# A Fourier layer, a soft mixture of experts and a Mish feed-forward on one core: shrunk spectra put in order at PSUM, second-stage chunks set one by one, forward spectra turned on chip

## The chip, the cores and the metric

The kernel runs on one core of a Trainium2 chip. The metric is the device time of one execution in microseconds (us), the median over several. The core has five engines with an instruction stream each: TensorE (PE; its weight loads are shown as PEld), VectorE (DVE), ScalarE (ACT), GpSimd (POOL) and SyncE (SP), which here only issues DMAs. They tell each other by semaphores that a result is there or a buffer is free. Matrix products land in PSUM; the rest of the work lies in SBUF and, between stages, in DRAM.

## The reference

Three layers follow each other. x is 8 batches of 3072 positions by 256 features, in float32; the weights of the last layer are 64-bit.

```python
X = np.fft.rfft(x, axis=1)                      # layer 1, per batch
Yr = Xr @ w_r - Xi @ w_i + b_r
Yi = Xr @ w_i + Xi @ w_r + b_i
Yr = sign(Yr) * max(abs(Yr) - 0.01, 0)          # shrink, Yi likewise
y = np.fft.irfft(Yr + 1j * Yi)

logits = y @ phi                                # layer 2, 32 slots = 8 experts x 4
d = softmax over all 24576 positions of logits; slot_input = d.T @ y
slot_out = relu(slot_input @ w1) @ w2           # per expert
c = softmax over the 32 slots of logits; z = c @ slot_out

h = z @ w_in; g = h * tanh(softplus(h)); out = g @ w_out    # layer 3
```

## The kernel before

The transform of 3072 points is split in two stages, 64 x 48. Per batch, `stage1` multiplies x by the 64-point matrix in six pieces, the result goes to DRAM (`sdr`, `store_a`) and comes back by position (`bt`, `load_b`) as four groups of 8 frequencies each. A group is numbered k, 32 in all. For a group, `stage2` makes the second-stage products in six chunks (two halves h of the features; chunks of 3, 3 and 2 frequencies, p0 = 0, 3, 6). ACT rounds each chunk out of PSUM to the high part xh, DVE makes the rest xl. `linear` then takes six steps per group, (eh, m) with eh = 0, 1 and m = 0, 1, 2: six products each (high by high, low by high, high by low, over the two halves), which read all chunks of the group. The step m = 0 leaves a sum k1, copied out by ACT; for m = 1 and 2 DVE adds k1 to the products (p), ACT makes the two shrinking halves (cl and p again), and GpSimd (DVE in the last group) subtracts them into the shrunk spectrum yt. The tile p has two buffers, cl has one.

From yt come two things. `project` multiplies by phi (pp) and DVE turns the result (phat) for the inverse transform of the logits (`inv1` to `inv2`). `ytrans` transposes yt in 128 x 128 blocks for later (tr, copied to y), reading every sixth column. Once per batch the logits are reduced (`smax1` to `smax3`, `csoft1`, `cexp`, `csoft2`, on dx, cm, lg), the weights d go through a forward transform (`fwd1` makes dps and dm, `d_load` fetches it as dd, `fwd2` makes dt, `dturn` turns it to dh), and `slots` sums d.T @ spectrum (sps). The part c goes to DRAM (`ctrans`, c_d). In between, the 64-bit weights of layer 3 are converted to float32 in pieces (`conv`, on DVE and GpSimd). After the last batch come the experts (`Experts.run`) and the feed-forward part (`ffn`, the matmuls at L868 and L910).

The order is written out by hand: each piece of work is put into a list with a position, and the list is sorted. The position counts groups: linear step i of group k stands at k + i / 6. The table `PA` holds the other offsets:

```python
at(k + PA["s2"] + PA["s2d"] * i, stage2, k, h, p0)   # i-th chunk of group k
at(k + i / 6, linear, k, i // 3, i % 3)
at(k + PA["pj"], project, k)
```

Each engine then works strictly along its own part of that list. PSUM is a ring of eight tiles (`psp`) in this part of the program.

Of the kernel before, what the change touches and what calls it, by code (L numbers as in the profile page):

```python
# [21 lines left out]
NP = 32  # L22
# [9 lines left out]
def constants():  # L32

    n1 = np.arange(R1, dtype=np.float64)
    n2 = np.arange(R2, dtype=np.float64)
    f1 = np.zeros((R1, R1))
    t = np.zeros((96, NP, 96))
    w = 2.0 * np.pi / SEQ
    f1[:, 0], f1[:, 1] = 1.0, np.where(n1 % 2 == 0, 1.0, -1.0)
    for pos in range(47):  # L40
        k, r = (R1 * (pos + 1), 0) if pos < 23 else (R1 // 2 + R1 * (pos - 23), R2)
        a = w * np.mod(n2 * k, SEQ)
        t[r:r + R2, 0, pos] = np.cos(a)
        t[r:r + R2, 0, 48 + pos] = -np.sin(a)
    t[0:R2, 0, 47] = 1.0
    t[0:R2, 0, 95] = np.where(n2 % 2 == 0, 1.0, -1.0)
    for q in range(1, NP):
        ang = 2.0 * np.pi * np.mod(n1 * q, R1) / R1
        f1[:, 2 * q], f1[:, 2 * q + 1] = np.cos(ang), -np.sin(ang)
        for k2 in range(R2):  # L50
            a = w * np.mod(n2 * (q + R1 * k2), SEQ)
            sg = 1.0 if k2 < R2 // 2 else -1.0
            t[0:R2, q, k2] = np.cos(a)
            t[R2:96, q, k2] = np.sin(a)
            t[0:R2, q, 48 + k2] = -sg * np.sin(a)
            t[R2:96, q, 48 + k2] = sg * np.cos(a)
    fd = np.kron(f1, np.eye(2))
    sel = np.tile(np.eye(NS), (4, 1))
    m = np.arange(128).reshape(4, 4, 2, 4)
    order = m.transpose(1, 0, 2, 3).reshape(-1)  # L60
    big = np.concatenate([fd, fd.T[order], np.eye(128), sel, np.tile(f1, (2, 1))], axis=1)
    tt = t.transpose(2, 1, 0)
    t3 = np.concatenate([t[:, :, 0:48] + t[:, :, 48:96], t], axis=2)
    both = np.concatenate([t3.reshape(96, -1), tt.reshape(96, -1)], axis=1)
    return np.ascontiguousarray(big.astype(np.float32)), np.ascontiguousarray(both.astype(np.float32))
# [3 lines left out]
def body(ctx, tc, x, w_r, w_i, b_r, b_i, phi, w1, w2, w_in, w_out, cbig, ct, out, dbg=None, stop=False):  # L69
# [53 lines left out]
    cs_t = {}  # L123

    x_t, b_t, xh_t, xl_t, yt_t, y_t, pt_t, k1_t = {}, {}, {}, {}, {}, {}, {}, {}
    sdr, spt, ddr, ch, a_t = {}, {}, {}, {}, {}
    XC = 512
    na = N2 * D // XC

# [94 lines left out]
    def stage2(k, h, p0):  # L224
# [15 lines left out]
        nc.scalar.activation(out=xh, in_=ps, func=AF.Copy)  # L240
        nc.vector.tensor_sub(part(xl_t[k]), ps, xh.bitcast(F32))  # L241
        if g == 0 and p0 == 0:
            for t in (xh_t[k], xl_t[k]):
                nc.vector.tensor_copy(t[:, h, 3 * NC:3 * NC + 48].rearrange("p (a r) -> p a r", r=2),
                                      t[:, h, 95:144:48][:, None, :].to_broadcast([128, 24, 2]).bitcast(F32))

    def linear(k, eh, m):
        if eh == 0 and m == 0:
            pool, tag = (bp, "b") if k >= NK - 2 else (yq, "yq") if k >= NK - 4 else (ytp, "yt")
            yt_t[k] = pool.tile([128, 2, 8, 2, 48], F32, tag=tag, name="yt")  # L250
        xh, xl, yt = xh_t[k], xl_t[k], yt_t[k]
        src, (wh, wl) = ((0, wsp["a"]), (2, wsp["b"]), (1, wsp["c"]))[m]
        w, nq = (NC + 2, 9) if m == 0 and k % 4 == 0 else (NC, 8)
# [11 lines left out]
                nc.tensor.matmul(full[:, 0:48 * nq].rearrange("p (q f) -> p q f", f=48), lhsT=ww[:, h, es], rhs=spec(xx, h), start=n == 0, stop=n == 5)  # L265
                n += 1
        if m == 0:
            k1_t[eh] = lp.tile([128, NC + 2], F32, tag="k1", name="k1")
            nc.scalar.activation(out=k1_t[eh][:, 0:w], in_=ps, func=AF.Copy)
            if w > NC:  # L270
                cs_t[eh] = cs = sm.tile([128, 2, 2], F32, tag="cs", name="cs")
                for i, sc in ((0, 0.5), (1, -0.5)):
                    nc.scalar.activation(out=cs[:, i], in_=k1_t[eh][:, NC:w], func=AF.Relu, scale=sc, bias=half[:, i, eh:eh + 1])
            return
        ri = m - 1
        p = lp.tile([128, 8, 48], F32, tag="p", name="p")
# [697 lines left out]
```

## Time and profile before

| | us |
|---|---|
| median of 3 runs | 1934.07 (1930.87 to 1936.53) |
| the profiled execution | 1935.8 |
| its span, first to last instruction | 1934.0 |
| PE busy in the span | 1875.3 (97%) |
| DVE busy | 1163.1 (60%) |
| ACT busy | 860.5 (44%) |
| GpSimd busy | 195.3 (10%) |

The span has two parts. Up to about 676 us lie the layers 1 and 2 with the experts; from there on the feed-forward part runs, whose matmuls at L910 and L868 hold most of the chain that ended last. A busy share over the whole span says little of the first part: it has to be read stretch by stretch. In the rows further down, a line is `engine line operation out<-in`; idle time stands with the engine that waited and what ended the wait.

### The profile page before, as it was taken

How to read it: one execution, taken by the hardware profiler on the slowest of the kernel's cores; microseconds unless marked ns; L12 is line 12 of the kernel's file. 1: busy time of each engine (PE TensorE's matmuls, PEld its weight loads, DVE VectorE, ACT ScalarE, POOL GpSimd, SP SyncE). 2: the span in 40 equal slices, each digit the busy share in tenths (PEclk: the TensorE clock that was granted, in tenths of full speed). 3: DMA queues.
4: the chain of work that ended last, by engine and by line, in shares of the span. 5: the costliest groups of instructions: out<-in, count | busy, mean ns of one | idle time of the engine just before them, and what ended most of it. 6: DMA issues, size and time to landing. Idle time of an engine off the chain costs nothing.

```text
span 1934.0 us, 29831 instructions
## 1 busy us (share of the span) xinstructions
PE 1875.3 (97%) x12106; PEld 1569.4 (81%) x12106; DVE 1163.1 (60%) x1810; ACT 860.5 (44%) x1380; POOL 195.3 (10%) x247
## 2 busy tenths in 40 slices
PE   6899999998998899999999999999999999999999
PEld 4687787777887488888888888888888888888887
DVE  3355655655566476666666666666666666666665
ACT  2666666665754243333333333333333333333332
POOL 0333333332332000000000000000000000000000
PEclk9999999999999999999999999999999999999999
DMA  9867777775663920020020020002002001000000
GB/s 246 235 150 173 168 184 177 170 185 132 161 167 107 343 74 22 23 55 22 12 55 23 23 55 23 23 12 55 22 23 55 22 19 48 22 23 22 23 22 23
DMA packets 96905, 164.28 MB, mean 85 GB/s; under 512 B 28784, under 2 KB 58096, under 8 KB 94848
## 3 DMA queue, kind: packets, MB, share of 16 engines
q1 hardware_dynamic: 93808, 155.13, 29.2%
q0 software_dynamic: 1792, 4.76, 0.8%
q10 hardware_dynamic: 1168, 2.49, 0.5%
q8 instruction: 95, 1.56, 0.3%
q14 instruction: 42, 0.34, 0.1%
HBM read 98.78 MB, written 63.57 MB: 84 GB/s over the span
## 4 chain that ended last, share of the span: by engine, by line
PE 88%; DMA 4%; DVE 3%; ACT 2%; issue 2%; POOL 1%; SPq 0%; POOLq 0%; ACTq 0%; DVEq 0%
PE o L910 56%; PE h L868 9%; PE l L265 8%; PE s L233 6%; PE tr L318 2%; PE s L201 2%; DMA dd<-ddr 2%; DMA bt<-sdr 1%; PE pp L296 1%; DMA xc<-in_x_dram 1%; PE sps L496 1%; POOL yt L285 1%; PE dt L478 1%; ACT cl L283 1%; PE iu L307 1%
## 5 line engine op out<-in xcount | busy, mean ns | idle before, releaser
L910 PE MATMUL o<-whl,gh 128*128 128x512 f32 x3072 | 1082.9, 395 | 0.0
L910 PE MATMUL o<-whl,gl 128*128 128x256 f32 x3072 | 827.9, 280 | 0.0
L881 ACT ACTIVATE g<-h 128x1024 f32<-128x1024 f32 (+1 forms) x385 | 394.2, 1025 | 747.8 <-PE h L868 738.0
L910 PEld LDWEIGHTS o<-whl,gh 128*128 128x128 f32 x3072 | 566.5, 188 | 121.5
L910 PEld LDWEIGHTS o<-whl,gl 128*128 128x128 f32 x3072 | 578.5, 188 | 31.5
L894 DVE TENSOR_TENSOR gl<-g,gh 128x1024 fp32r<-128x1024 f32 x383 | 468.9, 1224 | 29.2 <-DVE gh L887 1.4
L887 DVE CAST gh<-g 128x1024 fp32r<-128x1024 f32 (+1 forms) x385 | 265.8, 690 | 352.6 <-ACT g L881 352.6
L868 PE MATMUL h<-ctt,mst 128*128 128x512 f32 x768 | 240.7, 394 | 1.5 <-ACT g L881 1.0
L233 PE MATMUL s<-tall,bt 96*128 96x144 f32 x1024 | 143.0, 301 | 23.0 <-DMA bt<-sdr 12.1
L233 PEld LDWEIGHTS s<-tall,bt 96*128 96x128 f32 x1024 | 138.6, 202 | 31.0 <-issue 26.4
L241 DVE TENSOR_TENSOR xl<-s,xh 128x432 fp32r<-128x432 f32 (+1 forms) x192 | 94.6, 550 | 113.6 <-ACT xh L240 113.3
L285 POOL TENSOR_TENSOR yt<-cl,p 128x384 f32<-128x384 f32 x124 | 125.2, 1010 | 352.6 <-ACT p L284 220.2
L868 PEld LDWEIGHTS h<-ctt,mst 128*128 128x128 f32 x768 | 121.0, 188 | 19.7 <-ACT g L881 1.8
L283 ACT ACTIVATE cl<-p,tup 128x384 f32<-128x384 f32 x124 | 76.3, 615 | 134.0 <-DVE p L277 98.1
L918 DVE TENSOR_TENSOR os<-o,os 128x256 f32<-128x256 f32 x192 | 76.5, 419 | 77.2 <-ACT os L917 77.2
L277 DVE TENSOR_TENSOR p<-l,k 128x384 f32<-128x384 f32 x128 | 70.6, 553 | 85.2 <-PE l L265 61.9
L240 ACT ACTIVATE xh<-s 128x432 fp32r<-128x432 f32 (+1 forms) x192 | 79.0, 503 | 36.7 <-PE s L233 36.3
L917 ACT ACTIVATE os<-o 128x256 f32<-128x256 f32 x192 | 73.4, 383 | 41.5 <-PE o L910 37.7
L284 ACT ACTIVATE p<-p,tlo 128x384 f32<-128x384 f32 x124 | 76.3, 615 | 4.0
L201 PE MATMUL s<-xc,f 64*64 64x512 f32 x384 | 56.6, 650 | 9.6 <-DMA xc<-in_x_dram 9.5
L318 PEld LDWEIGHTS tr<-cb,yt 128*128 128x128 f32 x384 | 55.4, 235 | 12.0 <-issue 4.5
L318 PE MATMUL tr<-cb,yt 128*128 128x128 f32 x384 | 62.2, 306 | 0.0
(187 smaller groups left out, 1392.1 us busy)
## 6 DMA issues: line engine op xcount, KB each, us to landing
sdr<-a SPq DMA_DIRECT2D x96, 256.0 KB, 3.8
bt<-sdr SPq DMA_DIRECT2D x32, 768.0 KB, 8.5
out_dram<-os SPq DMA_DIRECT2D x47, 512.0 KB, 2.6
xc<-in_x_dram SPq DMA_DIRECT2D x90, 256.0 KB, 5.4
ctt<-c_d SPq DMA_DIRECT2D x28, 384.0 KB, 7.0
w1t<-in_moe_w_dram SPq DMA_DIRECT2D x6, 1024.0 KB, 7.4
c_d<-chl SPq DMA_DIRECT2D x14, 384.0 KB, 2.8
w2t<-in_moe_w_dram SPq DMA_DIRECT2D x5, 1024.0 KB, 12.2
```

The lines of the kernel that those rows point to most:

```text
L201: nc.tensor.matmul(ps[h][64 * c:64 * c + 64], lhsT=f64[hs], rhs=t[hs, XC * c:XC * c + XC], start=True, stop=True, tile_position=(64 * h, 6 ...
L233: nc.tensor.matmul(ps[:, i], lhsT=b_t[k][:, p0 + i, h * 128:(h + 1) * 128], rhs=t_m[:, 8 * g + p0 + i, :], start=True, stop=True)
L241: nc.vector.tensor_sub(part(xl_t[k]), ps, xh.bitcast(F32))
L265: nc.tensor.matmul(full[:, 0:48 * nq].rearrange("p (q f) -> p q f", f=48), lhsT=ww[:, h, es], rhs=spec(xx, h), start=n == 0, stop=n == 5)
L283: nc.scalar.activation(out=cl, in_=p, func=AF.Relu, bias=tup[:, ri, eh:eh + 1])
L285: nc.gpsimd.tensor_sub(yt[:, eh, :, ri, :], cl, p)
L318: nc.tensor.transpose(ps[:, i, eh], yt[:, eh].rearrange("p q r f -> p (q r f)")[:, 2 * c + i::6], ident)
L868: nc.tensor.matmul(ps[:, i], lhsT=mst[:, f * 128:f * 128 + 128], rhs=ct_t[b][:, 4 * m:4 * m + 4].rearrange("p n t -> p (n t)"), start=True ...
L881: nc.scalar.activation(out=v(g), in_=v(h), func=AF.Mish)
L887: nc.vector.tensor_copy(v(gh), v(g))
L894: nc.vector.tensor_sub(gl, g, gh.bitcast(F32))
L910: nc.tensor.matmul(o, lhsT=a[:, i, ts], rhs=w, start=f == 0 and n == 0, stop=f == 15 and n == 1)
```

## The change

Three edits in one. First, the shrunk spectrum yt is laid out in the order in which `ytrans` reads it, six blocks of 128 columns in a row: the reads of the linear step's PSUM by ACT (k1) and DVE (p) take every sixth column (`split6`), GpSimd writes runs of eight into yt, `ytrans` reads 128 neighbouring columns, `project` reads runs of 16, and a table of constants changes its row order to match. The two extra columns (cs, and the bins in `stage2`) are now read from PSUM by ACT and DVE. Second, the six chunks of `stage2`, which stood as one block before the last linear steps of the group ahead, are placed one in front of each linear step. Third, for the batches before the last, `fwd1` turns its result by two DVE transposes and `d_load` by eight PE transposes with one ACT and one DVE copy, as the last batch did already; the DMA to DRAM and the DMA back are gone, and `d_load` stands a little later.

```diff
-    tt = t.transpose(2, 1, 0)
+    r = np.arange(16)
+    tt = t.transpose(2, 1, 0)[np.concatenate([6 * r + m for m in range(6)])]
...
         if g == 0 and p0 == 0:
-            for t in (xh_t[k], xl_t[k]):
-                nc.vector.tensor_copy(t[:, h, 3 * NC:3 * NC + 48].rearrange("p (a r) -> p a r", r=2),
-                                      t[:, h, 95:144:48][:, None, :].to_broadcast([128, 24, 2]).bitcast(F32))
+            bins = full.rearrange("p q r f -> p (q r f)")[:, 95:144:48][:, None, :].to_broadcast([128, 24, 2])
+            xh, xl = (t[:, h, 3 * NC:3 * NC + 48].rearrange("p (a r) -> p a r", r=2) for t in (xh_t[k], xl_t[k]))
+            nc.scalar.activation(out=xh, in_=bins, func=AF.Copy)
+            nc.vector.tensor_sub(xl, bins, xh.bitcast(F32))
+
+    def split6(t):
+        return t[:, 0:NC].rearrange("p (q f m) -> p m q f", q=8, m=6)
...
-            yt_t[k] = pool.tile([128, 2, 8, 2, 48], F32, tag=tag, name="yt")
+            yt_t[k] = pool.tile([128, 2, 6, 128], F32, tag=tag, name="yt")
...
         if m == 0:
-            k1_t[eh] = lp.tile([128, NC + 2], F32, tag="k1", name="k1")
-            nc.scalar.activation(out=k1_t[eh][:, 0:w], in_=ps, func=AF.Copy)
+            k1_t[eh] = lp.tile([128, 6, 8, 8], F32, tag="k1", name="k1")
+            nc.scalar.activation(out=k1_t[eh], in_=split6(full), func=AF.Copy)
...
-        p = lp.tile([128, 8, 48], F32, tag="p", name="p")
-        nc.vector.tensor_add(p.rearrange("p q f -> p (q f)"), ps, k1_t[eh][:, 0:NC])
-        cl = lp.tile([128, 8, 48], F32, tag="cl", bufs=1, name="cl")
+        o = yt[:, eh].rearrange("p m (q r f) -> p m q r f", q=8, r=2)[:, :, :, ri]
+        p = lp.tile([128, 6, 8, 8], F32, tag="p", name="p")
+        nc.vector.tensor_add(p, split6(full), k1_t[eh])
+        cl = lp.tile([128, 6, 8, 8], F32, tag="cl", bufs=1, name="cl")
+        pf, cf = (t.rearrange("p m q f -> p (m q f)") for t in (p, cl))
...
-            nc.scalar.activation(out=cl, in_=p, func=AF.Relu, bias=tup[:, ri, eh:eh + 1])
-            nc.scalar.activation(out=p, in_=p, func=AF.Relu, scale=-1.0, bias=tlo[:, ri, eh:eh + 1])
-            nc.gpsimd.tensor_sub(yt[:, eh, :, ri, :], cl, p)
+            nc.scalar.activation(out=cf, in_=pf, func=AF.Relu, bias=tup[:, ri, eh:eh + 1])
+            nc.scalar.activation(out=pf, in_=pf, func=AF.Relu, scale=-1.0, bias=tlo[:, ri, eh:eh + 1])
+            nc.gpsimd.tensor_sub(o, cl, p)
...
-            v = yt[:, eh].rearrange("p q r f -> p q (r f)")
+            v = yt[:, eh].rearrange("p m (q j) -> p q m j", q=8)
             for a in range(3):
-                nc.tensor.matmul(ps[32 * a:32 * a + 32], lhsT=ph[:, eh, :], rhs=v[:, :, 32 * a:32 * a + 32],
+                nc.tensor.matmul(ps[32 * a:32 * a + 32], lhsT=ph[:, eh, :], rhs=v[:, :, 2 * a:2 * a + 2],
...
-                nc.tensor.transpose(ps[:, i, eh], yt[:, eh].rearrange("p q r f -> p (q r f)")[:, 2 * c + i::6], ident)
+                nc.tensor.transpose(ps[:, i, eh], yt[:, eh, 2 * c + i], ident)
...
-        dm = cp.tile([128, 32, N2] if last else [128, N2, NS], F32, tag="st" if last else "chl", bufs=1 if last else 2, name="dm")
+        dm = cp.tile([128, 32, N2], F32, tag="st" if last else "chl", bufs=1 if last else 2, name="dm")
         for i in range(2):
             ps = psum([128, 12, NS], "dps")
             nc.tensor.matmul(ps, lhsT=f1, rhs=d[:, 12 * i:12 * i + 12], start=True, stop=True)
-            if last:
-                nc.vector.transpose(out=dm.rearrange("p q n -> p n q")[:, 12 * i:12 * i + 12], in_=ps)
-            else:
-                nc.scalar.activation(out=dm[:, 12 * i:12 * i + 12], in_=ps, func=AF.Copy)
-        if last:
-            ch[b, 0] = dm
-            return
-        ddr[b] = dram.tile([NP, 96, NS], F32, tag="ddr", bufs=2, name="ddr")
-        nc.sync.dma_start(out=ddr[b].rearrange("q (r n) s -> (q r) n s", r=4), in_=dm)
+            nc.vector.transpose(out=dm.rearrange("p q n -> p n q")[:, 12 * i:12 * i + 12], in_=ps)
+        ch[b, 0] = dm
...
         if b < NB - 1:
-            dd = cp.tile([96, NP, NS], F32, tag="dd", name="dd")
-            nc.sync.dma_start(out=dd, in_=ddr[b].rearrange("q p s -> p q s"))
-            ch[b, 0] = [dd[:, q] for q in range(NP)]
-            return
+            both = cp.tile([96, 2, 4, 128], F32, tag="dd", name="dd")
...
-            dd = yp.tile([96, 4, 128], F32, tag="y", name="dd")
+            dd = both[:, a] if b < NB - 1 else yp.tile([96, 4, 128], F32, tag="y", name="dd")
...
-PA = dict(..., s2=-1.1, s2d=0.0002, ..., dl=2.05, ...)
+PA = dict(..., s2=-1.03, s2d=1 / 6, ..., dl=2.2, ...)
```

What this does to the order shows best on the two engines that empty PSUM. The first place is DVE around the start of a group in the fourth batch: xl is the low part of a chunk of `stage2`, p the sum of a linear step, cva a step of `conv`, phat the turned projection. Before:

```order
L277 TENSOR_TENSOR p<-l,k_2767 128x384 x2
L241 TENSOR_TENSOR xl<-s_2809,xh 128x432
L241 TENSOR_TENSOR xl<-s_2815,xh 128x432
L241 TENSOR_TENSOR xl<-s_2821,xh 128x288
L241 TENSOR_TENSOR xl<-s_2826,xh 128x432
L241 TENSOR_TENSOR xl<-s_2832,xh 128x432
L241 TENSOR_TENSOR xl<-s_2838,xh 128x288
L544 TENSOR_SCALAR cva<-cvs 128x256
L546 SCALAR_TENSOR_TENSOR cva<-cvs,cva 128x256
L277 TENSOR_TENSOR p<-l,k_2853 128x384
```

And the same place now:

```order
L283 TENSOR_TENSOR p<-l,k_2774 128x384
L242 TENSOR_TENSOR xl<-s_2798,xh 128x288
L283 TENSOR_TENSOR p<-l,k_2774 128x384
L242 TENSOR_TENSOR xl<-s_2827,xh 128x432
L541 TENSOR_SCALAR cva<-cvs 128x256
L242 TENSOR_TENSOR xl<-s_2859,xh 128x432
L543 SCALAR_TENSOR_TENSOR cva<-cvs,cva 128x256
L283 TENSOR_TENSOR p<-l,k_2843 128x384
L306 STREAM_TRANSPOSE phat<-pp 96x256
L545 SCALAR_TENSOR_TENSOR cva<-cvc,cva 128x256
L242 TENSOR_TENSOR xl<-s_2910,xh 128x288
L283 TENSOR_TENSOR p<-l,k_2843 128x384
```

Where two p followed each other and six xl came in a block, each p now has an xl ahead of it. The second place is ACT at the same time: xh is the high part of a chunk, cl and p are the two shrinking halves, k the sum k1, a a piece of `stage1`. Before:

```order
L283 ACTIVATE cl<-p,tup 128x384
L284 ACTIVATE p<-p,tlo 128x384
L240 ACTIVATE xh<-s_2809 128x432
L240 ACTIVATE xh<-s_2815 128x432
L240 ACTIVATE xh<-s_2821 128x288
L240 ACTIVATE xh<-s_2826 128x432
L240 ACTIVATE xh<-s_2832 128x432
L240 ACTIVATE xh<-s_2838 128x288
L269 ACTIVATE k_2853<-l 128x386
```

And now:

```order
L290 ACTIVATE cl<-p,tup 128x384
L291 ACTIVATE p<-p,tlo 128x384
L241 ACTIVATE xh<-s_2798 128x288
L208 ACTIVATE a<-s_2804 128x512
L208 ACTIVATE a<-s_2805 128x512
L290 ACTIVATE cl<-p,tup 128x384
L291 ACTIVATE p<-p,tlo 128x384
L241 ACTIVATE xh<-s_2827 128x432
L274 ACTIVATE k_2843<-l 128x384
```

The block of six xh is gone; one xh stands behind each pair cl and p. The third place is DVE in the reductions of a batch, where dx, cm and lg are passes over 768 columns and st is a copy of the inverse transform. Before:

```order
L311 COPY st<-iu 128x8x24
L383 TENSOR_TENSOR dx<-lg,mb 128x768
L391 TENSOR_REDUCE cm<-lg 128x24
L392 TENSOR_TENSOR lg<-lg,cm 128x768
L277 TENSOR_TENSOR p<-l,k_3169 128x384 x2
```

And now:

```order
L242 TENSOR_TENSOR xl<-s_3150,xh 128x432
L318 COPY st<-iu 128x8x24
L390 TENSOR_TENSOR dx<-lg,mb 128x768
L398 TENSOR_REDUCE cm<-lg 128x24
L399 TENSOR_TENSOR lg<-lg,cm 128x768
L242 TENSOR_TENSOR xl<-s_3187,xh 128x432
L283 TENSOR_TENSOR p<-l,k_3176 128x384
L242 TENSOR_TENSOR xl<-s_3206,xh 128x288
L283 TENSOR_TENSOR p<-l,k_3176 128x384
L439 STREAM_TRANSPOSE dm<-dps 128x12x32 x2
```

The same passes now stand between two xl, and the two transposes dm are new on DVE behind them.

## Rows read from the trace of the kernel before

**Rows 1.** Stretches: length; busy us of PE, PEld, DVE, ACT, POOL; PE's clock; DMA.

```profile
178.40:551.90 373.50, 359.68 (x3035) 288.75 (x3030) 214.42 (x499) 243.88 (x501) 123.03 (x154) 0.98 0.68 172
252.40:324.80 72.40, 70.99 (x616) 56.74 (x609) 42.88 (x102) 48.76 (x101) 24.57 (x31) 1.00 0.71 175
551.90:676.00 124.10, 112.17 (x1065) 82.11 (x1057) 71.39 (x165) 55.80 (x110) 26.30 (x31) 0.97 0.57 199
676.00:1934.00 1258.00, 1253.01 (x6912) 1082.03 (x6912) 796.26 (x966) 465.72 (x581) 0.00 (x0) 1.00 0.10 31
```

**Rows 2.** Waits of PE up to 676 us: total, times, longest.

```profile
PE s L233 <- DMA bt<-sdr: 12.1, 3, 6.5
PE dt L478 <- DMA dd<-ddr: 9.9, 7, 2.5
...
PE s L233 <- ACT dm L435: 2.5, 5, 0.9
```

**Rows 3.** Timeline of PE: start us, us from first start to last end.

```profile
255.58 0.49 PE L413 MATMUL ctps<-cb,lg 128*128 128x128 f32 x3
255.91 0.70 PE L318 MATMUL tr<-cb,yt 128*128 128x128 f32 x4
...
270.74 1.89 PE L318 MATMUL tr<-cb,yt 128*128 128x128 f32 x12
272.38 0.42 PE L265 MATMUL l<-xh,ch 128*128 128x384 f32 x1
...
278.54 4.08 PE L233 MATMUL s<-tall,bt 96*128 96x144 f32 x32
282.36 0.43 PE L265 MATMUL l<-xh,ah 128*128 128x384 f32 x1
...
283.52 0.34 PE L265 MATMUL l<-xh,bh 128*128 128x384 f32 x1
...
658.30 1.16 PE L769 MATMUL htp<-cb,hs 128*128 128x128 f32 x8
```

**Rows 4.** Waits of SP's queue: total, times, longest.

```profile
SPq L440 <- ACT dm L435: 80.0, 7, 26.6
```

**Rows 5.** The tile dm: ns min/median/max; DVE's is the last batch's.

```profile
L433 DVE STREAM_TRANSPOSE dm<-dps x2: 1143/1152/1161, 635.9 to 636.9; 128x384 f32<-128x384 f32 x2
```

**Rows 6.** The tile dd in the last batch.

```profile
L458 ACT ACTIVATE dd<-td x1: 593/593/593, 638.8 to 638.8; 96x512 f32<-96x512 f32 x1
```

**Rows 7.** Timeline of ACT, around 320 us.

```profile
317.95 0.61 ACT L283 ACTIVATE cl<-p,tup 128x384 f32<-128x384 f32 x1 [1.11 <-POOL yt L285]
...
319.12 2.37 ACT L240 ACTIVATE xh<-s 128x432 fp32r<-128x432 f32 x6
...
325.09 0.61 ACT L283 ACTIVATE cl<-p,tup 128x384 f32<-128x384 f32 x1 [1.45 <-DVE p L277]
```

**Rows 8.** Timeline of DVE, the same stretch.

```profile
319.66 0.61 DVE L241 TENSOR_TENSOR xl<-s,xh 128x432 fp32r<-128x432 f32 x1 [2.55 <-ACT xh L240]
320.18 0.30 DVE L244 CAST xh<-xh 128x48 fp32r<-128x48 f32 x1
...
324.44 0.55 DVE L277 TENSOR_TENSOR p<-l,k 128x384 f32<-128x384 f32 x1
```

**Rows 9.** The tile lg: reductions of a batch on DVE.

```profile
L383 DVE TENSOR_TENSOR dx<-lg,mb x9: 544/952/961, 144.8 to 634.3; 128x768 f32<-128x768 f32 x7, 128x384 f32<-128x384 f32 x2
L391 DVE TENSOR_REDUCE cm<-lg x8: 928/942/946, 146.4 to 634.8; 128x24 f32<-128x768 f32 x8
...
L405 DVE TENSOR_TENSOR lg<-lg,cs__2511 x1: 958/958/958, 240.9 to 240.9; 128x768 f32<-128x768 f32 x1
```

**Rows 10.** The tile p: GpSimd's subtraction.

```profile
L285 POOL TENSOR_TENSOR yt<-cl,p x124: 983/1007/1215, 50.1 to 615.5; 128x384 f32<-128x384 f32 x124
```

**Rows 11.** DVE's copies out of PSUM: the tiles mst and y.

```profile
L853 DVE CAST mst<-mr x2: 682/687/692, 675.2 to 675.9; 128x512 fp32r<-128x512 f32 x2
...
L321 DVE COPY y<-tr x3: 675/676/692, 639.8 to 642.5; 128x512 f32<-128x512 f32 x3
```

More of the change, by code (lines that the diff above doesn't have):

```diff
@@ L125, in body @@
     x_t, b_t, xh_t, xl_t, yt_t, y_t, pt_t, k1_t = {}, {}, {}, {}, {}, {}, {}, {}
-    sdr, spt, ddr, ch, a_t = {}, {}, {}, {}, {}
+    sdr, spt, ch, a_t = {}, {}, {}, {}
     XC = 512
@@ L272, in linear @@
                 for i, sc in ((0, 0.5), (1, -0.5)):
-                    nc.scalar.activation(out=cs[:, i], in_=k1_t[eh][:, NC:w], func=AF.Relu, scale=sc, bias=half[:, i, eh:eh + 1])
+                    nc.scalar.activation(out=cs[:, i], in_=full[:, NC:w], func=AF.Relu, scale=sc, bias=half[:, i, eh:eh + 1])
             return
         ri = m - 1
-        p = lp.tile([128, 8, 48], F32, tag="p", name="p")
-        nc.vector.tensor_add(p.rearrange("p q f -> p (q f)"), ps, k1_t[eh][:, 0:NC])
-        cl = lp.tile([128, 8, 48], F32, tag="cl", bufs=1, name="cl")
+        o = yt[:, eh].rearrange("p m (q r f) -> p m q r f", q=8, r=2)[:, :, :, ri]
[3 more added lines that the diff above has]
+        pf, cf = (t.rearrange("p m q f -> p (m q f)") for t in (p, cl))
         if k == NK - 1:
-            nc.vector.tensor_scalar(cl, p, tlo[:, ri, eh:eh + 1], thi[:, ri, eh:eh + 1], op0=ALU.max, op1=ALU.min)
-            nc.vector.tensor_sub(yt[:, eh, :, ri, :], p, cl)
-        else:
-            nc.scalar.activation(out=cl, in_=p, func=AF.Relu, bias=tup[:, ri, eh:eh + 1])
-            nc.scalar.activation(out=p, in_=p, func=AF.Relu, scale=-1.0, bias=tlo[:, ri, eh:eh + 1])
-            nc.gpsimd.tensor_sub(yt[:, eh, :, ri, :], cl, p)
+            nc.vector.tensor_scalar(cf, pf, tlo[:, ri, eh:eh + 1], thi[:, ri, eh:eh + 1], op0=ALU.max, op1=ALU.min)
+            nc.vector.tensor_sub(o, p, cl)
+        else:
+            nc.scalar.activation(out=cf, in_=pf, func=AF.Relu, bias=tup[:, ri, eh:eh + 1])
+            nc.scalar.activation(out=pf, in_=pf, func=AF.Relu, scale=-1.0, bias=tlo[:, ri, eh:eh + 1])
+            nc.gpsimd.tensor_sub(o, cl, p)
         if m == 2 and k % 4 == 0:
             cs = cs_t.pop(eh)
-            nc.gpsimd.tensor_sub(yt[:, eh, 0, :, 47], cs[:, 0], cs[:, 1])
+            nc.gpsimd.tensor_sub(yt[:, eh, 5, 7:16:8], cs[:, 0], cs[:, 1])
     def project(k):
@@ L795, in run @@
                 nc.vector.tensor_copy(sot[:, h, 16 * g:16 * g + 16].rearrange("p (j i) -> p j i", i=SPE), src)
-PA = dict(y=20, s1=-5.89, s1d=0.3402, lb=-1.91, s2=-1.1, s2d=0.0002, pj=1.18, yt=2.24, ytd=0.0002, tu=0.482, i2=1.17, m1=1.17, m2=1.34, m3=1.51, f1=1.84, c1=1.58, ce=1.58, ds=2.47, dl=2.05, c2=2.57, f2=2.46, sl=3.2, rc=0.3, cx=3.24, cxd=0.0002, x0=-0.79, x1=0.05, ytl=1.05, x2=1.3, x3=2.7)
+PA = dict(y=20, s1=-5.89, s1d=0.3402, lb=-1.91, s2=-1.03, s2d=1 / 6, pj=1.18, yt=2.24, ytd=0.0002, tu=0.482, i2=1.17, m1=1.17, m2=1.34, m3=1.51, f1=1.84, c1=1.58, ce=1.58, ds=2.47, dl=2.2, c2=2.57, f2=2.46, sl=3.2, rc=0.3, cx=3.24, cxd=0.0002, x0=-0.79, x1=0.05, ytl=1.05, x2=1.3, x3=2.7)
 TAIL = {
```

## The prediction

> **What bounds it now.** I read the table of stretches first, then the waits of PE, then PE's timeline, and last the timelines of ACT and DVE in one place. From 676 us on, the feed-forward part runs with PE busy 1253.0 of 1258.0 us, and no edit reaches it [rows 1]. The time can change only before that. The first 95.7 us wait for inputs (PE's longest wait for bt, 6.5 us, is among them [rows 2]) and hold too little of the changed work to move it. From 178.4 to 551.9 us lie five batches of equal work, 373.5 / 5 = 74.7 us each, with PE busy 359.7 / 5 = 71.9; the quietest batch took 72.4 us with PE busy 71.0 [rows 1]. So PE is the bound there, and what it idles is known by name: 9.9 us for dd, 2.5 for dm, 12.1 for bt, of which 5.6 come after the first stretch [rows 2]. ACT is busy 243.9 / 5 = 48.8 us a batch, DVE 42.9. The reader is to see a full engine with two others that are two thirds full, and to ask whether those two stay free enough once their work is strung differently.
>
> **What PE saves.** In ytrans the stationary operand is read now with a step of six words. Twelve such transposes took 272.38 - 270.74 = 1.64 us, 0.137 each; three transposes of words in a row took 255.91 - 255.58 = 0.33, 0.11 each [rows 3]. The change gives ytrans 128 words in a row, so it should go at the second rate: 12 x 0.027 = 0.32 us a group, 1.3 a batch. Against this stand eight new transposes per batch (td), 8 x 0.11 = 0.9, with a little for the entry. Thirty-two second-stage matmul passes took 282.36 - 278.54 = 3.82 us in one block [rows 3]; cut in six they are the same passes, and a break costs at most a filling of the pipe (0 to 0.1 us, twenty more per batch; I take 0.2 us a batch in all). PE's own work stays at 71.0 - 1.3 + 0.9 + 0.2 = about 70.8 us a batch.
>
> **What PE no longer waits for.** The trip of dm through DRAM goes, its two DMAs leave SP's queue, and with them SP's wait of 80.0 us over seven batches for ACT's dm [rows 4], behind which the stores of a, the loads of xc and the loads of bt stood. All 9.9 us for dd go, and probably the 2.5 and the 5.6. What is late next: td waits for two DVE transposes that write with a step of 24 words, 2 x 1.15 us [rows 5], against two ACT copies before. Between dps and td PE has two chunks and two linear steps, 2 x (0.72 + 1.16) = 3.8 us (six passes of 0.12, and a step from 282.36 to 283.52 [rows 3]), with a stage-1 piece and a projection beside them; so td is covered as long as DVE comes to dm in time, and costs up to 2.3 us a batch if not. fwd2 then waits for one ACT copy (0.59 [rows 6]) and one DVE copy of as many words as y (0.68 [rows 11]), and has twelve transposes, a chunk and a step to hide them. ACT is thereby about even, DVE gets 2.3 + 0.7 = 3.0 us a batch more.
>
> **What the other engines pay.** Both work strictly in the order written. Before, DVE does two p in a row and then six xl; after, one xl stands ahead of every p, and on ACT one xh stands behind every pair cl, p. An m = 1 or 2 step is then a relay. DVE's p starts; ACT's cl starts 325.09 - 324.44 = 0.65 us later; cl and p together take 319.12 - 317.95 = 1.17; then xh; DVE's xl starts 319.66 - 319.12 = 0.54 after xh; the next DVE work starts 0.52 later [rows 7, 8]. Only then can the next p start: 0.65 + 1.17 + 0.54 + 0.52 = 2.9 us from p to p (a little less where the chunk is one of two columns instead of three), while PE needs 0.5 to 0.7 us for a chunk and 1.16 for a step. In each such step ACT idles from the end of xh to cl, about 0.14 + 0.5 + 0.65 = 1.3 us, sixteen times a batch: 20.6 us on top of its 48.8, together 69.4. Two places add to that. Where dx, cm and lg stand between two xl, three passes of 0.95 us each [rows 9] lie in the relay: +2.8. Where csoft2 stands (a reduction like cm, 0.94, and a product, 0.96 [rows 9], with st and the turns of dh), ACT has 0.9 us of its own work to do meanwhile: about +2.6. Sum: 74.8 us a batch, say 75, against 70.8 of PE.
>
> PE may run ahead of the relay in the middle of a group (eight PSUM tiles), but at a group's start its first step needs the last xl. At a step with nothing between, the last xl ends 0.65 + 1.17 + 0.54 + 0.4 = 2.8 us after the start of the p that it follows, and PE wants it after a chunk, a step, a chunk and four matmuls, 0.5 + 1.16 + 0.7 + 0.7 = 3.1; a lag of a few tenths is allowed there, and 1 to 2.5 us where a stage-1 piece or dps lies between. Time that the relay loses after csoft2 or smax3 is therefore not made up in the next group. I take 75 us.
>
> **Costs that no row shows.** GpSimd's subtraction writes runs of 8 words instead of 48. It takes 1.0 us now [rows 10]. The next cl waits for it (one buffer), but xh, xl and p lie between, 1.7 us: up to about half as much again costs nothing, and a gain would be worth nothing. I take 1.0. The reads of PSUM with a step of six words by ACT (k1) and DVE (p): the nearest row is the copy of mst, 512 words read with a step of four, 0.687 us on DVE, against 0.676 for as many in a row [rows 11]. I take no cost; the far end is a doubling, as for DVE's transpose with a strided output. The moving operand of project falls into runs of 16 words; it is timed by 256 columns in both, and I take nothing, with 0 to 0.1 us a group as bounds.
>
> [...]
>
> **The sum.** Relay: (75.0 - 74.7) x 6.6 batches from 95.7 to about 590 us = +2. From 551.9 to 676 us PE idles 124.1 - 112.2 = 11.9 us [rows 1]; there the last dd wait (2.5 [rows 2]) goes and some forty transposes are 1 us cheaper; with a little of the slower clock that followed the wait, -4.5. Together -2.5 us. The profiled execution took 1935.8 us, 1.7 over the median of the runs shown, so it becomes 1933.3, and the median about 1932.
>
> **Rivals.** (1) The relay is hidden: PE's other blocks (projections, transposes, slot sums) give ACT and DVE the time to catch up, and PE stays full. Then a batch takes 70.8 plus some 0.7 of waits that stay: (71.5 - 74.7) x 6.6 - 4.5 = -25.6, 1908 us. For it: ACT and DVE have over 23 us of idle time a batch. Against it: that idle time is not free, since 20.6 of ACT's is now bound in the relay.
> (2) Slower: the same relay, but with what I left out. The weights of the last layers are converted (conv) in steps that DVE and GpSimd pass to each other, and these stand in DVE's order too; PE's stops at group starts also bring the slower clock, as the granted 0.97 to 0.98 in the stretches with long waits shows, against 1.00 in the quietest batch [rows 1]. At 78 us a batch: 3.3 x 6.6 - 3 = +19, 1953 us. It decides from 76 us on.
> (3) Strided reads of PSUM take twice as long: 16 p of 0.55 us [rows 8] more per batch in the relay, 8.8 x 6.6 = +58, 1990 us. The row of mst speaks against it. [...]
> (4) The transposes do not get cheaper, because the step was not the reason: the eight htp, whose step is eight words, took 1.16 us with their drain, hardly more than a row of words would [rows 3]. In the relay's case this costs nothing but 1 us at the end, in rival 1 it costs 1.3 x 6.6 = 9 us: 1917. It shifts, and does not decide.
>
> **Chances.** Relay near 75 us: 0.42, own range 1920 to 1946. Rival 1 (with 4): 0.30. Rival 2: 0.23. Rival 3: 0.05. A measurement of this kernel tells about 0.3%, 6 us, from no change. Of the relay's 0.42 I give 0.14 to faster by more than that, 0.20 to no difference, 0.08 to slower. Faster 0.30 + 0.14 = 0.44, same 0.20, slower 0.08 + 0.28 = 0.36. The range must hold both neighbours: 1904 to 1956.
>
> **What will show it.** Right: tr at 0.11 us each; no dd wait and no wait of SP for dm; ACT waiting for DVE's p far more than now, DVE for xh after each pair; PE stopped at the start of groups by xl. If PE waits there for nothing and a batch takes 71 us, rival 1 holds. If p or k1 take 0.8 us and more, rival 3. I am wrong altogether if the first stage's end does not lie between 646 and 700 us.

## The result

The changed kernel took 1950.16 us (median of four runs, 1949.18 to 1950.89), the kernel before 1933.05 in the same comparison (four runs, 1930.87 to 1936.53). The ratio is 1.0087, interval 1.0069 to 1.0104: slower by 0.9%, where 1932 and rather faster than slower had been forecast. The time lies in the range (1904 to 1956); the direction is wrong. It is close to the 1953 us of the second rival, but by luck: that rival needed 78 us a batch, and a batch took 75.6.

The profiled execution took 1950.63 us (span 1948.8). To compare equal work, the stretches are cut at the same events in each kernel: the first slot-sum matmul of batch 0 and of batch 5 (0.6 us behind each), and 3.4 us ahead of the feed-forward's first o. For the kernel before these are the cuts of [rows 1]. Stretches of the changed kernel (start:end, length, busy us of PE, PEld, DVE, ACT and POOL, granted clock, DMA share, GB/s):

```profile
179.80:558.00 378.20, 363.45 (x3074) 282.40 (x3069) 226.14 (x506) 240.81 (x508) 123.33 (x155) 1.00 0.63 159
558.00:689.30 131.30, 117.71 (x1098) 84.14 (x1088) 76.34 (x173) 57.54 (x115) 26.36 (x31) 0.96 0.51 183
689.30:1948.80 1259.50, 1254.66 (x6911) 1083.13 (x6910) 795.77 (x965) 465.38 (x580) 0.00 (x0) 1.00 0.10 31
```

Against [rows 1] the five batches took 4.7 us more (378.2 - 373.5; 75.6 instead of 74.7 each), the end of the first part 7.2 more (131.3 - 124.1), the start 1.4 (179.8 - 178.4) and the feed-forward part 1.5. That is 14.8 us, the difference of the spans. The batches' granted clock rose from 0.98 to 1.00, so it is not the clock that lengthened them. PE's busy time there rose as well, from 359.68 to 363.45 us, though its matmuls got cheaper: the same ones take 351.36 in e1 below. So a part of the waiting stands in the busy time, and not only in the idle time.

The waits of [rows 2] for dd and dm, and that of [rows 4], are gone. PE now waits most of all for ACT's xh (engine, line, what it waited for: total, times, longest):

```profile
PE l L270 <- ACT xh L241: 15.4, 18, 1.8
```

What ACT and DVE wait for shows the relay. In the kernel before, ACT's cl waited for DVE's p, and DVE's xl for ACT's xh, for this long in all:

```profile
ACT cl L283 <- DVE p L277: 98.1, 72, 3.5
...
DVE xl L241 <- ACT xh L240: 113.3, 46, 11.8
```

In the changed kernel it is:

```profile
ACT cl L290 <- DVE p L283: 165.8, 117, 4.5
...
DVE xl L242 <- ACT xh L241: 218.5, 152, 11.4
```

One turn of it, on DVE around 400 us in the changed kernel (start us, us, what; in brackets the idle time before it and what ended it):

```profile
399.26 0.57 DVE L242 TENSOR_TENSOR xl<-s,xh 128x432 fp32r<-128x432 f32 x1
399.75 0.41 DVE L543 SCALAR_TENSOR_TENSOR cva<-cvs,cva 128x256 int32<-128x256 int32 x1
400.08 0.55 DVE L283 TENSOR_TENSOR p<-l,k 128x384 f32<-128x384 f32 x1
...
402.31 0.46 DVE L242 TENSOR_TENSOR xl<-s,xh 128x288 fp32r<-128x288 f32 x1 [1.09 <-ACT xh L241]
402.69 0.37 DVE L481 STREAM_TRANSPOSE dh<-dt 128x192 f32<-128x192 f32 x1
402.99 0.52 DVE L283 TENSOR_TENSOR p<-l,k 128x384 f32<-128x384 f32 x1
```

The same stretch on ACT:

```profile
400.72 0.61 ACT L290 ACTIVATE cl<-p,tup 128x384 f32<-128x384 f32 x1 [4.47 <-DVE p L283]
401.37 0.61 ACT L291 ACTIVATE p<-p,tlo 128x384 f32<-128x384 f32 x1
401.89 0.39 ACT L241 ACTIVATE xh<-s 128x288 fp32r<-128x288 f32 x1
403.60 0.62 ACT L290 ACTIVATE cl<-p,tup 128x384 f32<-128x384 f32 x1 [1.32 <-DVE p L283]
```

And PE in it, in the first linear step of a group:

```profile
400.59 0.34 PE L270 MATMUL l<-xh,al 128*128 128x384 f32 x1
402.33 0.44 PE L270 MATMUL l<-xh,ah 128*128 128x384 f32 x1 [1.41 <-ACT xh L241]
```

Read them together: p at 400.08, cl at 400.72, xh at 401.89, xl at 402.31, the next p at 402.99, 2.91 us in all. ACT has been idle 4.47 us before cl, since DVE stood in csoft2's work (the passes over lg that end ahead of the first row shown); its xh, whose matmuls had ended at 398.57 us, stands behind cl and p. So PE's fourth product of the step, the first that needs the second half of xh, stands 1.41 us. ACT kept to the order written: this xh could have run 3.3 us before 401.89 and did not.

### The profile page after: what moved, and what is told of

Same layout as the page of the kernel before. It is cut to its first block, busy times and chain, and to the rows that moved or that the text cites. A ratio compares the mean times of both kernels' runs of the same rounds, so it can differ in the third digit from the quotient of the medians.

```text
span 1948.8 us, 29919 instructions
## 1 busy us (share of the span) xinstructions
PE 1891.2 (97%) x12162; PEld 1566.1 (80%) x12162; DVE 1177.5 (60%) x1815; ACT 855.4 (44%) x1389; POOL 195.7 (10%) x247
## 4 chain that ended last, share of the span: by engine, by line
PE 73%; ACT 11%; DVE 8%; issue 3%; DMA 1%; POOL 0%; ACTq 0%; POOLq 0%; SPq 0%; DVEq 0%
PE o L907 55%; PE h L865 9%; ACT cl L290 3%; PE l L270 2%; DVE p L283 2%; ACT xh L241 2%; ACT p L291 2%; DVE xl L242 2%; ACT y L330 2%; PE s L234 1%; ACT a L208 1%; PE sps L493 1%; PE s L202 1%; PE pp L303 1%; PE tr L325 1%
## 5 line engine op out<-in xcount | busy, mean ns | idle before, releaser
L242 DVE TENSOR_TENSOR xl<-s,xh 128x432 fp32r<-128x432 f32 (+1 forms) x192 | 106.4, 555 | 218.7 <-ACT xh L241 218.5
L234 PE MATMUL s<-tall,bt 96*128 96x144 f32 x1024 | 168.7, 300 | 13.4 <-issue 6.3
L234 PEld LDWEIGHTS s<-tall,bt 96*128 96x128 f32 x1024 | 148.8, 197 | 37.6 <-issue 18.7
L241 ACT ACTIVATE xh<-s 128x432 fp32r<-128x432 f32 (+1 forms) x192 | 93.8, 490 | 27.3 <-PE s L234 27.3
L270 PE MATMUL l<-xh,ah 128*128 128x384 f32 (+1 forms) x128 | 53.7, 419 | 15.5 <-ACT xh L241 15.4
L208 ACT ACTIVATE a<-s 128x512 f32<-128x512 f32 x90 | 48.9, 596 | 16.3 <-PE s L202 8.4
```

The source lines that it names most:

```text
L234: nc.tensor.matmul(ps[:, i], lhsT=b_t[k][:, p0 + i, h * 128:(h + 1) * 128], rhs=t_m[:, 8 * g + p0 + i, :], start=True, stop=True)
```

## Experiments

Every kernel was timed against the kernel before in three rounds. Ratios have 95% intervals; the batch is a fifth of the stretch between the two slot-sum marks and the end is the stretch from the second mark on, both of the profiled execution.

| kernel | median us | ratio to before | batch | end |
|---|---|---|---|---|
| before | 1933 | 1 | 74.7 | 124.1 |
| changed | 1950.2 | 1.0087 (1.0069 to 1.0104) | 75.6 | 131.3 |
| e1 changed, chunks in a block | 1913.7 | 0.9894 (0.9880 to 0.9909) | 70.7 | 123.4 |
| e2 before, chunks spread | 1982.8 | 1.0253 (1.0227 to 1.0279) | 80.4 | 134.0 |
| e3 before, layout | 1929.3 | 0.9984 (0.9968 to 1.0001) | 73.3 | 123.5 |
| e4 before, turn on chip | 1918.0 | 0.9919 (0.9904 to 0.9934) | 71.8 | 120.7 |
| e5 changed, last four groups in a block | 1941.8 | 1.0040 (1.0026 to 1.0054) | 76.1 | 121.4 |
| e7 changed, cl later | 1915.5 | 0.9899 (0.9876 to 0.9922) | 71.9 | 121.8 |
| e8 changed, xl later | 1911.0 | 0.9875 (0.9852 to 0.9898) | 70.8 | 122.3 |
| e9 changed, less conv | 1933.2 | 0.9999 (0.9985 to 1.0013) | 73.3 | 125.9 |
| e10 xl later, less conv | 1909.0 | 0.9886 (0.9860 to 0.9912) | 70.4 | 120.8 |

**The three parts apart.** First the change without its spread:

```diff
-s2=-1.03, s2d=1 / 6
+s2=-1.1, s2d=0.0002
```

> The changed kernel with the second stage's six chunks of a group back in one block ahead of the last linear step of the group before (as in the kernel before); layout and on-chip turn stay. Theory A, the relay (chunk in front of every linear step ties ACT and DVE together and PE waits for them): ACT's waits for DVE's p fall from 165.8 us to about 100, PE's 15.4 us for xh go, and what remains is PE's own saving (32 x 0.32 - 7 x 0.9 = 4 us) and the waits for dd, dm and part of bt that the on-chip turn removed (up to 18 us): 1911 to 1925 us. Theory B, the turn on chip costs the time (two DVE transposes of 1.15 us, an ACT and a DVE copy, eight transposes per batch, in front of the forward transforms): the spread is innocent, 1942 to 1952 us. Theory C, the two share it: 1926 to 1941 us.

Then each part alone on the kernel before. The spread (e2):

```diff
-s2=-1.1, s2d=0.0002
+s2=-1.03, s2d=1 / 6
```

> The kernel before with one edit: the second stage's chunks one in front of each linear step; old layout, and the forward spectra still turned through DRAM. Theory A, the relay: it is slower than before by at least what the whole change lost, since nothing of the change's savings is there: 1950 to 1970 us, with ACT waiting for DVE's p 150 us or more. Theory B, the turn on chip: no loss, 1928 to 1938 us.

The layout (e3) is the diff of `tt`, `stage2`'s bins, `linear`, `project` and `ytrans`:

```diff
+            k1_t[eh] = lp.tile([128, 6, 8, 8], F32, tag="k1", name="k1")
+            nc.scalar.activation(out=k1_t[eh], in_=split6(full), func=AF.Copy)
...
-                nc.tensor.transpose(ps[:, i, eh], yt[:, eh].rearrange("p q r f -> p (q r f)")[:, 2 * c + i::6], ident)
+                nc.tensor.transpose(ps[:, i, eh], yt[:, eh, 2 * c + i], ident)
```

> The kernel before with the layout alone: spectra ordered by part where PSUM is read (k1, p), runs of 128 words for the transposes of yt; chunks in a block, turn through DRAM. 384 transposes at 0.11 instead of 0.137 us are 10 us of PE's time. Theory A (PE bounds the blocked kernel): 1921 to 1927 us. If the gain is hidden behind the waits for bt and dd instead: 1930 to 1936 us.

The turn on chip (e4) is the diff of `fwd1` and `d_load`, with their new place:

```diff
-        dm = cp.tile([128, 32, N2] if last else [128, N2, NS], F32, tag="st" if last else "chl", bufs=1 if last else 2, name="dm")
+        dm = cp.tile([128, 32, N2], F32, tag="st" if last else "chl", bufs=1 if last else 2, name="dm")
...
-dl=2.05
+dl=2.2
```

> The kernel before with the on-chip turn alone (DVE transposes for dm, PE transposes and copies for dd, the last step placed at 2.2 as in the changed kernel); chunks in a block, old layout. Theory A, the relay is the loss and the turn a gain: the waits for dd (9.9 us), dm (2.5) and part of bt (5.6) go, 7 x 0.9 us of transposes come: 1918 to 1930 us. Theory B, the turn is the loss: 1945 to 1955 us.

Theory A holds in e1, e2 and e4, though e2 lies 13 us above its range. In e1 ACT's wait for p falls to 90.2 us and DVE's for xh to 94.1. The turn alone is worth 15 us, with the layout on top 19 (e1); the spread costs 36 us on top of both (1950.2 - 1913.7) and 50 alone. In the spread without the turn the DRAM trip takes part in the loss; PE's wait for dd was 9.9 us over seven times before [rows 2], and is in e2:

```profile
PE dt L478 <- DMA dd<-ddr: 25.7, 6, 6.0
```

The layout alone is between the two expectations and cannot be told from nothing (its interval reaches 1.0001). In the batches its PE time is there, though: from e4 to e1, where PE is no longer stopped by the trip, a batch falls by 1.1 us, as 48 transposes at 0.027 less would have it (1.3). In all, e1 is 4.4 us ahead of e4 and not 10, since its end is 2.7 us longer; why was not looked into. In e3 PE waits 12.9 us in all for dd, against 9.9 before, which takes a part of the gain.

e1's five batches, the same columns as above, show the full PE that the prediction had counted at 70.8 us a batch (353.6 / 5 = 70.7):

```profile
175.60:529.20 353.60, 351.36 (x3075) 280.81 (x3069) 226.99 (x502) 240.27 (x505) 123.76 (x154) 1.00 0.67 170
```

**The loop itself.** e1 takes away the relay and the chunks' place at once. Two kernels keep every chunk where the change has it, and every operation, and open the loop at one link each. In e7 cl, p and yt of a step follow the next chunk's xh on ACT:

```diff
+            def rest():
                 nc.scalar.activation(out=cf, in_=pf, func=AF.Relu, bias=tup[:, ri, eh:eh + 1])
                 nc.scalar.activation(out=pf, in_=pf, func=AF.Relu, scale=-1.0, bias=tlo[:, ri, eh:eh + 1])
                 nc.gpsimd.tensor_sub(o, cl, p)
...
+            late.append(rest)
```

> The changed kernel, chunks spread as there, with one thing moved: cl, p and GpSimd's subtraction of a linear step are issued behind the next chunk's high part (ACT: xh, cl, p instead of cl, p, xh). No work is added or removed. Now xh never waits for DVE's p, so the loop p, cl, p, xh, xl, p is open. Theory A, it is the loop that costs: most of the 36 us between the spread and the blocked form come back, 1910 to 1925 us, and ACT's waits for p and DVE's for xh fall by half or more. Theory B, it is the chunks' place as such (PE changes operand every few matmuls, and a chunk's xh and xl are needed sooner after they are made): 1940 to 1952 us.

In e8 xl follows the next p on DVE:

```diff
-        nc.vector.tensor_sub(part(xl_t[k]), ps, xh.bitcast(F32))
+        late.append(lambda: nc.vector.tensor_sub(part(xl_t[k]), ps, part(xh_t[k]).bitcast(F32)))
+        if k <= 0 or h == 1 and p0 == 6:
+            flush()
...
         nc.vector.tensor_add(p, split6(full), k1_t[eh])
+        flush()
```

> The loop opened at the other link: the changed kernel with a chunk's xl issued on DVE behind the next p instead of ahead of it (the last chunk of a group keeps its place, since the next linear step needs it). Theory A, the loop costs: a good part comes back, less than by the other link, because one step in six still has the old order: 1915 to 1932 us. Theory B, the place of the chunks as such: 1940 to 1955 us, since xl comes later.

Both give back all of it, e8 a little more than expected (1911.0). The chunks' place is innocent: theory B falls. DVE of e8, at the place shown above for the changed kernel:

```profile
376.79 0.56 DVE L295 TENSOR_TENSOR p<-l,k 128x384 f32<-128x384 f32 x1 [0.15 <-PE l L281]
377.26 0.60 DVE L242 TENSOR_TENSOR xl<-s,xh 128x432 fp32r<-128x432 f32 x1
...
379.03 0.46 DVE L242 TENSOR_TENSOR xl<-s,xh 128x288 fp32r<-128x288 f32 x1 [0.58 <-ACT xh L241]
379.41 0.37 DVE L494 STREAM_TRANSPOSE dh<-dt 128x192 f32<-128x192 f32 x1
379.70 0.52 DVE L295 TENSOR_TENSOR p<-l,k 128x384 f32<-128x384 f32 x1
```

p at 376.79 waits for PE alone, behind the same csoft2, and xl comes after it. From p to p it is still 2.91 us here, because this chunk is the group's last and keeps the old order; but ACT got its p one xl earlier, and PE runs through. The stretch of e8, with PE busy 353.6 of 354.2 us:

```profile
170.50:524.70 354.20, 353.55 (x3075) 282.15 (x3070) 229.49 (x506) 242.01 (x506) 125.37 (x154) 1.00 0.66 169
```

In part the expectation missed: that both waits fall by half. One link opened frees the engine behind it, the other keeps waiting where it costs nothing. In e7 ACT's wait for p falls to 39.2 us, DVE's for xh stays at 184.7:

```profile
ACT cl L299 <- DVE p L291: 39.2, 35, 2.0
...
DVE xl L242 <- ACT xh L241: 184.7, 128, 12.3
```

and in e8 it is the other way round:

```profile
ACT cl L303 <- DVE p L295: 112.9, 106, 2.2
...
DVE xl L242 <- ACT xh L241: 75.4, 71, 12.0
```

e7 is left with 71.9 us a batch. What its profile has more of is PE's wait for yt ahead of the projection, since cl comes later (in the changed kernel this row is 1.9 us, four times):

```profile
PE pp L314 <- POOL yt L301: 8.8, 10, 1.6
```

**The end.** e5 spreads groups 0 to 27 and puts only the last four in a block:

```diff
-            at(k + PA["s2"] + PA["s2d"] * i, stage2, k, h, p0)
+            at(k - 1.1 + 0.0002 * i if k >= NK - 4 else k + PA["s2"] + PA["s2d"] * i, stage2, k, h, p0)
```

> The changed kernel with the chunks spread for groups 0 to 27 and in one block for the last four groups (28 to 31) alone. From the last batch's first linear step to the feed-forward's first matmul the changed kernel took 122.2 us, the one with all chunks in a block 113.5. Theory A, the loss at the end is the relay in groups 28 to 31: 1938 to 1945 us. Rival: the end loses because ACT and DVE arrive there late, from the batches before: 1947 to 1953 us.

Theory A: the time lies in its range, and the end falls from 131.3 to 121.4 us, while the batches stay at 76. So the loss at the end is made there, in groups 28 to 31, not brought along.

**conv.** e9 takes four of conv's five steps on DVE and one of its two on GpSimd away:

```diff
-            p.tensor_tensor(c.bitcast(F32), hf, hf, op=ALU.mult)
...
-        elif step == 2:
+        elif step < 6:
+            return
+        elif step == 2:
...
-            p.tensor_tensor(c.bitcast(F32), a.bitcast(F32), c.bitcast(F32), op=ALU.add)
+            p.tensor_tensor(c.bitcast(F32), a.bitcast(F32), a.bitcast(F32), op=ALU.add)
```

> The changed kernel with less of conv: of its five steps on DVE four are left out (0.42 + 0.42 + 0.29 + 0.42 us) and of GpSimd's two one (0.61), so the converted weights are not the right ones. That is 1.55 us of DVE's work for each of 32 pieces, 50 us in all, four pieces a batch. Theory A, conv lies in DVE's waits for xh (117 us between 200 and 550): 1943 to 1951 us, the end a few us better. Rival (conv in DVE's order is part of the loop, piece by piece): up to 6 us a batch, 1910 to 1930 us; half of it: 1930 to 1940 us.

It is 17 us faster: theory A is refuted, and the time lies in the rival's middle case. A batch gains 2.3 us (75.6 to 73.3) and the end 5.4. Whether that is conv's own cost or its place in the loop, e10 tells, the same cut in the open loop of e8:

> The kernel with the loop opened on DVE (xl behind the next p) and with less of conv, the same steps left out as in the run on the changed kernel (so the converted weights are not the right ones). There conv's 50 us of DVE work were worth 17 us. Theory A, conv cost that time because it stood in the loop of p, cl, p, xh and xl: with the loop open PE is the bound and DVE's work is free, 1906 to 1912 us, no more than 4 us under the open loop's 1911. Rival, conv costs on its own account (ports, DMAs, DVE's load): again 12 us or more, 1890 to 1899 us.

There it is worth nothing that can be told: 1909.0 against 1911.0, with ratios to before of 0.9886 (0.9860 to 0.9912) and 0.9875 (0.9852 to 0.9898); the intervals leave room for some 5 us. So conv costs little or nothing by itself; its 17 us hang on the loop. The place above, around 400 us, shows how. There conv's L543 stands on DVE between xl and p, p starts 0.33 us later for it (399.75 to 400.08), and PE's stop is 1.41 us. In e9, which leaves that step out, the same stop is 0.37 us shorter:

```profile
393.61 0.45 PE L270 MATMUL l<-xh,ah 128*128 128x384 f32 x1 [1.04 <-ACT xh L241]
```

Not every wait of conv reaches PE. Around 590 us in the changed kernel, first GpSimd's square (cvc) has to wait for the DMA that writes the previous piece out of the same buffer:

```profile
589.89 0.61 POOL L540 TENSOR_TENSOR cvc<-cvs 128x256 f32<-128x256 f32 x1 [1.90 <-DMA wout_d<-cvc]
```

then DVE waits for that square in its order, with two xl and a p queued behind:

```profile
590.54 1.21 DVE L545 SCALAR_TENSOR_TENSOR cva<-cvc,cva 128x256 f32<-128x256 f32 x1 [2.04 <-POOL cvc L540]
```

then ACT waits for that p, with the next xh behind it:

```profile
593.88 0.62 ACT L290 ACTIVATE cl<-p,tup 128x384 f32<-128x384 f32 x1 [3.13 <-DVE p L283]
```

PE has other blocks in its order meanwhile (products of the reductions, a projection and transposes) and goes from one to the next without a stop:

```profile
590.70 2.40 PE L347 MATMUL lps<-v,cb 128*128 128x384 f32 x4
593.02 1.06 PE L303 MATMUL pp<-yt,ph 128*32 128x256 f32 x12
594.02 1.53 PE L325 MATMUL tr<-cb,yt 128*128 128x128 f32 x12
595.38 0.66 PE L234 MATMUL s<-tall,bt 96*128 96x144 f32 x4
```

## Why the prediction was wrong

**PE's saving: right.** The weight load of a transpose of yt fell from 237 to 141 ns (the kernel before, then the changed one; min/median/max):

```profile
L318 PEld LDWEIGHTS tr<-cb,yt x384: 209/237/243, 80.0 to 642.6; 128*128 128x128 f32 x192
...
L325 PEld LDWEIGHTS tr<-cb,yt x384: 137/141/143, 83.0 to 654.9; 128*128 128x128 f32 x192
```

Twelve of the transposes take 1.36 us (594.02 to 595.38 in the rows above), 0.113 each, where 0.11 had been forecast. The 0.1 us at most for a break in PE's products stands in the traces as well: behind a chunk the first product of a step is 0.27 us ahead of the second (282.36 to 282.63 in the kernel before, 585.21 to 585.48 in the changed one), and the second 0.18 ahead of the third, 0.09 us in all.

"PE's own work stays at about 70.8 us a batch" is what e1 and e8 measure, 70.7 and 70.8. Rival 4 falls: a step of six words was the reason in this layout.

**What PE no longer waits for: right** in place and size. e4 gains 15 us where 9.9 + 2.5 + 5.6 less 7 x 0.9 of new transposes would be 12. In the changed kernel dd and td are not among PE's waits of 0.7 us and more; dm on DVE takes 1.148 us, as [rows 5].

**Strided reads of PSUM: right**, rival 3 falls. p takes what it took in [rows 8], and GpSimd's subtraction, which now writes runs of eight, what it took in [rows 10] (the changed kernel; min/median/max ns):

```profile
L283 DVE TENSOR_TENSOR p<-l,k x128: 519/548/558, 45.7 to 635.6; 128x384 f32<-128x384 f32 x128
...
L292 POOL TENSOR_TENSOR yt<-cl,p x124: 987/1004/1209, 47.6 to 628.2; 128x384 f32<-128x384 f32 x124
```

For DVE's reads with a step of six words this trace shows no price: p has a median of 548 ns, against 557 in the kernel before. The forecast's far end, a doubling, had its model in DVE's transposes of 128 x 384 in the kernel before: 1152 ns for dm, from PSUM and written with a step of 24 words [rows 5], against 556 for v, from SBUF and in a row. The moving operand of project shows no price either: a product pp has a median of 379 ns in both kernels.

**The relay: right as a mechanism and in its sum, by two errors that cancel.** Its turn was put at 2.9 us, a little less with a chunk of two columns. With such a chunk it is 2.61 from p to p in the changed kernel, and 2.91 at the place around 400 us, where a dh stands between as well:

```profile
585.01 0.54 DVE L283 TENSOR_TENSOR p<-l,k 128x384 f32<-128x384 f32 x1
...
587.24 0.46 DVE L242 TENSOR_TENSOR xl<-s,xh 128x288 fp32r<-128x288 f32 x1 [1.49 <-ACT xh L241]
587.62 0.55 DVE L283 TENSOR_TENSOR p<-l,k 128x384 f32<-128x384 f32 x1
```

A batch was put at 75 and is 75.6. But the 74.8 were worked out with conv left out, and the relay without most of conv takes 73.3 (e9); conv then adds 2.3. That the 75 came out so near was luck. The prediction had named conv only as part of rival 2 and gave it no price of its own. That PE would be stopped by "the last xl" is mostly not what happened. It is xh, the high part of the second half, which stands behind cl and p on ACT, as PE's weight loads of the linear steps show (the changed kernel; total, times, longest):

```profile
PEld l L270 <- ACT xh L241: 22.3, 22, 2.1
...
PEld l L270 <- DVE xl L242: 7.7, 25, 0.5
```

**The step that failed is the end, "-4.5".** It was costed only with what goes: the last wait for dd, forty cheaper transposes and a little of the slower clock. The relay was carried "to about 590 us" against a batch of before, and so stood in this term at nothing. Measured: +7.2. Groups 28 to 31 are in the relay as all the others, and e5 shows that they are where the loss is made: with these four alone in a block the end is 9.9 us shorter. The first stage's matmuls, which elsewhere stand among the steps, are over by then; their last weight load starts at 531.7 us:

```profile
L202 PEld LDWEIGHTS s<-xc,f x384: 129/132/228, 6.3 to 531.7; 64*64 64x64 f32 x192
```

That they would have given ACT and DVE time is argued here and not tested. Two of the stops in the end are these, the first behind a transpose of the reductions on DVE (v, 0.98 us), the second behind smax3's three passes (PE):

```profile
587.26 0.44 PE L270 MATMUL l<-xh,ah 128*128 128x384 f32 x1 [1.26 <-ACT xh L241]
...
608.27 0.44 PE L270 MATMUL l<-xh,ah 128*128 128x384 f32 x1 [1.83 <-ACT xh L241]
```

Behind both the granted clock fell for a while, which rival 2 had expected of the batches (they show 1.00). Two stretches of 10 us of the changed kernel, the columns as above (the clock is the third last):

```profile
588.00:598.00 10.00, 9.89 (x59) 7.68 (x58) 5.90 (x13) 6.20 (x13) 4.13 (x6) 0.83 0.09 23
608.00:618.00 10.00, 9.68 (x83) 7.53 (x83) 7.74 (x14) 5.39 (x12) 4.68 (x6) 0.83 0.00 0
```

It fell a third time in the experts' matmuls hp, behind a stop of 1.05 us that e9 has as well, and there the same work with the fall and without it gives the price. In the changed kernel 48 of them run from 663.71 to 670.70, 6.99 us, at a granted clock of 0.76; in e9 they run from 646.59 to 651.88, 5.29 us, at 1.00 throughout. First the changed kernel, then e9:

```profile
663.71 7.05 PE L758 MATMUL hp<-w1t,sit 128*32 128x512 f32 x48 [1.05 <-DVE sit L645]
...
646.59 5.36 PE L759 MATMUL hp<-w1t,sit 128*32 128x512 f32 x48 [1.05 <-DVE sit L646]
```

So 1.7 us each time. The kernel before has two such falls in its end, one behind its last wait for dd (0.83 from 606 to 616 us) and one in hp (6.94 us). By this estimate the clock explains about 2 of the 7.2 us, and the relay's waits some 5, which is what a batch loses to the relay as well (75.6 us against 70.7 in e1). But a stop does not always bring the lower clock. In e9 the same step behind smax3 stands 1.81 us (PE's timeline):

```profile
592.36 0.44 PE L270 MATMUL l<-xh,ah 128*128 128x384 f32 x1 [1.81 <-ACT xh L241]
```

and the clock is 1.00 over its whole end (e9, the columns as above), against 0.96 in the changed kernel:

```profile
544.20:670.10 125.90, 112.30 (x1095) 81.09 (x1087) 70.32 (x157) 57.47 (x115) 24.00 (x28) 1.00 0.53 190
```

So of the 5.4 us that e9 gains in the end, the three falls that it does not have make up 5.1; beside them no price of conv is left to be seen there. The 9.9 us that e5 gains in the end are more than the relay's 5 for the same reason: its end has one such fall instead of three (hp, 6.70 us).

Of the 17.3 us between the 1933.3 forecast for the profiled execution and its 1950.6, this one term is 11.7. The batches account for 3.2, the start for 0.9 and the feed-forward part's entry for 1.5; these last two were not looked into further. Without the relay in groups 28 to 31 the end would gain less than 4.5 as well: it is 123.4 us in e1, 122.3 in e8 and 121.4 in e5, which is 0.7 to 2.7 less than before. Not settled is why one stop brings the lower clock and another does not.

**Why rival 1 had looked like a rival at all.** The forecast set the relay's 75 beside the 74.7 us of before and called it even. The 74.7 were 71 to 72 of PE, plus waits that this very change takes away. Seen so, the relay was worth 5 us a batch, 36 us in the kernel, and the change was a gain of 19 us hidden under it. Rival 1's 1908 us is close to the time of the open loop (1911.0), for which one operation changes its place on DVE.

## What to carry to other kernels

When a block of work is cut up and set between other steps, write down for two in-order engines who waits for whom from one step to the next. If the arrows close a loop through both, the loop's length is the price of each step, however idle the engines are (here 2.61 to 2.91 us a turn, and 75.6 us a batch against 70.8 with the loop open in e8); move one operation behind its neighbour on one engine, so that the arrow points a step back, and the loop is open. Price each part of a change against the bound without waits and not against the mean of before, and carry a loop on to the last place where it runs; everything that stands in the order of the two engines, from another job too, is part of its length.

## What the runs showed of the hardware

The stationary operand of a transpose of yt loaded in 237 ns where it was read with a step of six words, and in 141 as words in a row; in return no price showed in ACT's and DVE's reads of PSUM with a step of six words (k1 486 ns against 492, p 548 against 557) or in GpSimd's writes in runs of eight (1004 ns against 1007). The operands are float32, 128 x 128 for the load and 128 x 384 for the others. Work of 50 us on an engine that is busy 60% of the time cost 17 us in one order of its instructions (e9 against the changed kernel) and nothing that could be told in another (e10 against e8).
